# k and v held as two heads by 64 partitions instead of four heads by 32, in a two-stage attention followed by a token mixer

## The chip, the cores and the metric

The kernel runs on one core of a Trainium2 chip. The metric is the device time of the whole program in microseconds (us). Each kernel was run several times; a run is called fast here when it lies within 1.5% of the fastest run of the same kernel in the same call, and slow otherwise. The trace of the kernel before, from which its profile below is read, is of a run recorded as slow (165.15 us). Where ratios are quoted, they are the mean time of one kernel's fast runs over that of the other's fast runs of the same rounds, so they are not quite the ratio of the medians that stand beside them.

## The reference, cut to what matters

There are 8 batches, 8 heads, 576 positions and 64 channels per head, and 32 packed rows p per head.

```
p_packed = softmax(p k^T / 8) v          # 32 x 64 per head: "packed" rows
attn     = softmax(q p_packed^T / 8) p_packed   # 576 x 64 per head
x        = heads side by side            # 576 x 512 per batch
W_tok    = (x w_q)(x w_k)^T / 8          # 576 x 576
out      = relu(W_tok x) w_out           # float32
```

The change touches the first line only: the scores of the packed rows (p k^T) and the product of their softmax with v ("P times V").

## The kernel before

A batch goes through some twenty steps, and a fixed table decides the order in which the steps of neighbouring batches follow each other on every engine. k and v stand in SBUF with four heads on the 128 partitions: 32 partitions for each head, each with 18 consecutive rows, and the eight heads are two such groups G.

```python
NG, NP = 2, 4            # groups of heads, heads in a group
R, QP = 18, 32           # rows on a partition, partitions of a head
def rows(x, b):
    return x[b].rearrange("(G pos) (sh sl) d -> (pos sh) G sl d", G=NG, sl=R)

def sa(b, c):            # scores of the packed rows, one third c of the rows
    ...
    for r in range(NC3):
        for G in range(NG):
            for pos in range(NP):                        # one head at a time
                m = slice(pos * QP, (pos + 1) * QP)
                nc.tensor.matmul(ps[m, r, G], kT[:, r, G, m], pT[:, b, G * NP + pos],
                                 start=True, stop=True)
    ...                                                  # e1 = exp(scale * ps)

def pv(b, _):            # P times V, one row of each partition at a time
    ...
    for s in range(R):
        e1, r, par = st[b]["e1", s // KR], s % KR // 2, s % 2
        for G in range(NG):
            for pos in range(NP):
                m = slice(pos * QP, (pos + 1) * QP)
                nc.tensor.matmul(
                    ps[m, G, 0:Dh + 1], e1[m, r, G, par, :], v_sb[m, G, s, 0:Dh + 1],
                    start=s == 0 and G == 0, stop=s == R - 1, skip_group_check=True)
    ...
```

In a batch that is 72 matmuls for the scores (128 rows by 32 columns of weights, 64 moving columns) and 144 for P times V (32 by 32, 65 moving columns). Each has a weight load of its own. I call a load and its matmul a pair; the program has 2904.

The softmax here doesn't subtract the row's maximum and nothing guards it: scores larger than these inputs give would overflow.

## Time and profile before

| | before |
|---|---|
| median of 3 runs (lowest to highest) | 165.62 us (163.43 to 167.62) |
| span of the profiled run | 163.3 us |
| TensorE busy | 127.2 us (78%) |
| stops of the weight loads at multiples of 128 pairs | 10, together 25.5 us |
| matmul time spent at half clock | 20.5 us |

These lines of the page of the kernel before give the busy time of each engine, then rows of 40 equal slices of the span (4.1 us each; a digit is the busy share in tenths, and PEclk is the granted TensorE clock in tenths of full speed), then the DMA queue that moves instructions (packets, MB, share of 16 engines' time).

```profile
span 163.3 us, 6603 instructions
PE 127.2 (78%) x2904; PEld 87.3 (53%) x2904; DVE 81.6 (50%) x198; ACT 86.5 (53%) x176; POOL 67.4 (41%) x90
...
PE   6652895984979795999079992999929969999950
PEclk9997589699999999999759999699975999999997
DMA  5999999999249969987963989675960241274874
...
q8 instruction: 22, 0.36, 1.0%
```

TensorE is the busiest engine, but the row has holes at slices 19, 24 and 29 (counted from 0), and PEclk falls to 5 to 7 at or just after them. The chain of work that ended last, followed back through the span, as shares by engine and then by line:

```profile
## 4 chain that ended last, share of the span: by engine, by line
PE 70%; issue 14%; DMA 5%; DVE 4%; SPq 2%; ACT 1%; DVEq 0%; ACTq 0%
PE out_ps L430 20%; PE T_ps L221 10%; PE pv_ps L269 7%; PE e_ps L318 6%; DMA v_in<-in_v_dram 5%; PE warm_ps L205 4%; PE mix_ps L399 4%; PE e_ps L256 3%; PE aT_ps L339 3%; PE wk_ps L347 3%; PE wq_ps L358 2%; PE g_ps L371 2%; PE y_ps L380 2%; SPq L133 1%; DVE rs L326 1%
```

So 14% of the span is "issue": the engine waited for nothing that the profile shows. The timeline of the weight loads (PEld) around the largest hole, in columns start, length, engine, line, operation, tile, count and the idle time before it:

```profile
76.82 0.24 PEld L269 LDWEIGHTS <-e_2148 32*32 32x32 bf16 x19
77.10 0.10 PEld L430 LDWEIGHTS <-rest 128*128 128x128 bf16 x1
82.71 0.10 PEld L430 LDWEIGHTS <-rest 128*128 128x128 bf16 x1 [5.51 <-issue]
82.72 0.12 PEld L339 LDWEIGHTS <-a_2068 96*128 96x128 bf16 x1
```

The same stretch for the matmuls (PE):

```profile
75.61 0.78 PE L269 MATMUL pv_ps<-v_bf_83,e_2049 32*32 32x65 bf16 x48
76.20 0.57 PE L269 MATMUL pv_ps<-v_bf_83,e_2121 32*32 32x65 bf16 x48
76.59 0.59 PE L269 MATMUL pv_ps<-v_bf_83,e_2148 32*32 32x65 bf16 x48
77.10 0.39 PE L430 MATMUL out_ps<-wout_w,rest 128*128 128x512 bf16 x1
82.71 0.61 PE L430 MATMUL out_ps<-wout_w,rest 128*128 128x512 bf16 x1 [5.22 <-issue]
```

The engine stops between two matmuls of one output step: both weight loads read the tile rest, which was complete, and still the second comes 5.6 us after the first. Just before, 144 pairs of P times V had gone by in 1.4 us. Sorted by start, the weight loads make ten stops over 1 us that are no wait for data. They come after the pairs in this table (counted from 0), and all numbers differ by multiples of 128, to within two. Two more pauses of the loads, after pairs 113 and 354 (1.0 and 2.4 us), read "issue" in the rows of the loads too, but the rows of their matmuls name a cast of v on GpSimd and one of wqk on VectorE as what ended them: those are waits for data, and both rows have to be read.

| after pair | 223 | 478 | 606 | 862 | 990 | 1246 | 1629 | 2013 | 2397 | 2653 |
|---|---|---|---|---|---|---|---|---|---|---|
| stop, us | 3.28 | 1.14 | 2.55 | 1.41 | 1.32 | 1.99 | 5.61 | 3.14 | 3.37 | 1.69 |

Three stretches of 20 us: busy time of PE, PEld, DVE, ACT and POOL in this order (with the number of instructions), then the clock, the DMA share and GB/s.

```profile
60.00:80.00 20.00, 15.66 (x517) 11.48 (x513) 11.68 (x29) 11.15 (x24) 10.30 (x14) 0.99 0.94 217
80.00:100.00 20.00, 16.34 (x383) 12.05 (x384) 11.09 (x27) 11.48 (x25) 7.36 (x9) 0.84 0.78 192
100.00:120.00 20.00, 16.56 (x384) 12.29 (x384) 11.51 (x27) 11.05 (x23) 6.67 (x8) 0.91 0.81 190
```

### The profile page before, as it was taken

To read this page: it belongs to the slowest core of one execution; us is meant where nothing else is said; L and a number is where in the kernel's file an instruction comes from. 1 tells how busy PE (TensorE), PEld (TensorE's weight loads), DVE (VectorE), ACT (ScalarE), POOL (GpSimd) and SP (SyncE) were. 2 spreads that over 40 slices of the span, in tenths; PEclk is the share of its full clock that TensorE was granted. 3 is DMA by queue.
4 is the path that set the end of the run, shared out by engine and by line. 5 is a ranking of instruction groups with operands and counts; after the bars stand their busy time and mean duration, and the time that the engine had idled before them with its cause. 6 is when DMAs were issued, how large, how long until landed. Compare 5 with 4: busy or idle time off the path is not lost.

```text
span 163.3 us, 6603 instructions
## 1 busy us (share of the span) xinstructions
PE 127.2 (78%) x2904; PEld 87.3 (53%) x2904; DVE 81.6 (50%) x198; ACT 86.5 (53%) x176; POOL 67.4 (41%) x90
## 2 busy tenths in 40 slices
PE   6652895984979795999079992999929969999950
PEld 2332673463758564866058681866727548565410
DVE  5220366143858583785026872667604747761310
ACT  3133455512955691885036863578514755877740
POOL 7730559900592494089000890068004450540000
PEclk9997589699999999999759999699975999999997
DMA  5999999999249969987963989675960241274874
GB/s 146 338 382 247 403 370 322 322 248 214 46 116 287 187 151 176 208 285 191 227 135 96 311 199 206 144 276 134 145 197 5 51 111 43 68 201 120 227 212 139
DMA packets 16076, 32.20 MB, mean 197 GB/s; under 512 B 2736, under 2 KB 6064, under 8 KB 16048
## 3 DMA queue, kind: packets, MB, share of 16 engines
q1 hardware_dynamic: 11856, 23.99, 46.9%
q0 software_dynamic: 4192, 7.80, 27.7%
q8 instruction: 22, 0.36, 1.0%
q14 instruction: 6, 0.05, 0.1%
HBM read 30.15 MB, written 9.44 MB: 242 GB/s over the span
## 4 chain that ended last, share of the span: by engine, by line
PE 70%; issue 14%; DMA 5%; DVE 4%; SPq 2%; ACT 1%; DVEq 0%; ACTq 0%
PE out_ps L430 20%; PE T_ps L221 10%; PE pv_ps L269 7%; PE e_ps L318 6%; DMA v_in<-in_v_dram 5%; PE warm_ps L205 4%; PE mix_ps L399 4%; PE e_ps L256 3%; PE aT_ps L339 3%; PE wk_ps L347 3%; PE wq_ps L358 2%; PE g_ps L371 2%; PE y_ps L380 2%; SPq L133 1%; DVE rs L326 1%
## 5 line engine op out<-in xcount | busy, mean ns | idle before, releaser
L430 PE MATMUL out_ps<-wout_w,relu 128*128 128x512 bf16 x128 | 35.3, 392 | 0.0
L120 ACT ACTIVATE o_sb<-out_ps 128x512 f32<-128x512 f32 x28 | 16.7, 595 | 15.0 <-PE out_ps L430 13.3
L312 DVE COPY qT<-T_ps 128x768 bf16<-128x768 bf16 x24 | 13.3, 555 | 13.2 <-PE T_ps L221 13.1
L247 DVE COPY kT<-T_ps 128x768 bf16<-128x768 bf16 x24 | 13.0, 546 | 11.7 <-PE T_ps L221 11.1
L205 PE MATMUL warm_ps<-warm 128*128 128x512 bf16 x40 | 17.2, 464 | 1.2 <-DVE warm L185 1.2
L430 PEld LDWEIGHTS <-relu 128*128 128x128 bf16 x128 | 11.6, 103 | 7.9 <-issue 0.9
L318 PEld LDWEIGHTS <-qT 128*96 128x96 bf16 x192 | 13.3, 142 | 4.6 <-issue 3.5
L390 ACT ACTIVATE relu<-mix_ps 128x512 bf16<-128x512 f32 x24 | 13.6, 605 | 2.2 <-PE mix_ps L399 1.9
L341 DVE COPY aT<-aT_ps 128x384 bf16<-128x384 bf16 x24 | 8.5, 353 | 11.9 <-PE aT_ps L339 11.9
L120 ACT ACTIVATE wk<-wk_ps 96x128 bf16<-96x128 f32 x16 | 4.3, 271 | 15.0 <-PE wk_ps L347 14.9
L399 PE MATMUL mix_ps<-wqT,y 128*128 128x512 bf16 x32 | 10.9, 389 | 0.1
L273 DVE RECIPROCAL rec<-pv_ps 128x2 f32<-128x2 f32 x8 | 1.4, 171 | 18.5 <-PE pv_ps L269 18.5
L282 POOL TENSOR_TENSOR ppb<-pp,mask 128x256 bf16<-128x256 bf16 x16 | 10.5, 679 | 0.1
L221 PE MATMUL T_ps<-ident,q_bf 128*128 128x128 bf16 x108 | 10.0, 235 | 0.0
L318 PE MATMUL e_ps<-ppT_115,qT 128*96 128x64 bf16 x96 | 7.4, 226 | 3.2 <-issue 3.2
L221 PE MATMUL T_ps<-ident,k_bf 128*128 128x128 bf16 x108 | 9.4, 225 | 0.0
L347 PEld LDWEIGHTS <-aT 128*96 128x96 bf16 x96 | 7.8, 134 | 2.6 <-issue 0.4
L430 PE MATMUL out_ps<-wout_w,rest 128*128 128x512 bf16 x16 | 5.0, 394 | 5.2 <-issue 5.2
L118 DVE COPY o_sb<-out_ps 128x512 f32<-128x512 f32 x8 | 5.4, 671 | 7.1 <-PE out_ps L430 3.7
L221 PEld LDWEIGHTS <-k_bf 128*128 128x128 bf16 x108 | 7.3, 101 | 2.7 <-issue 0.8
L347 PE MATMUL wk_ps<-pqk,aT 128*96 128x64 bf16 x96 | 8.3, 214 | 0.1
L256 PE MATMUL e_ps<-pT,kT 128*32 128x64 bf16 x576 | 8.1, 199 | 0.3 <-DVE kT L247 0.3
(320 smaller groups left out, 287.6 us busy)
## 6 DMA issues: line engine op xcount, KB each, us to landing
v_in<-in_v_dram SPq DMA_DIRECT2D x7, 1152.0 KB, 8.4
out_dram<-o_sb SPq DMA_DIRECT2D x24, 192.0 KB, 2.6
k_bf<-in_k_dram POOLq DMA_DIRECT2D x6, 576.0 KB, 10.3
q_bf<-in_q_dram POOLq DMA_DIRECT2D x6, 576.0 KB, 8.2
out_dram<-o_sb SPq DMA_DIRECT2D x24, 128.0 KB, 2.5
out_dram<-o_sb SPq DMA_DIRECT2D x24, 64.0 KB, 2.2
k_in<-in_k_dram SPq DMA_DIRECT2D x3, 384.0 KB, 3.9
v_in<-in_v_dram SPq DMA_DIRECT2D x3, 384.0 KB, 7.7
```

What stands on the lines that cost most here:

```text
L120: nc.scalar.activation(o, i, COPY)
L205: nc.tensor.matmul(ps, warm[:, 0:P], warm, start=True, stop=True)
L221: nc.tensor.transpose(ps[:, r, G, :], xc[:, G, r].rearrange("a x d -> a (x d)"), ident)
L247: nc.vector.tensor_copy(kT, ps)
L256: nc.tensor.matmul(ps[m, r, G], kT[:, r, G, m], pT[:, b, G * NP + pos], start=True, stop=True)
L269: nc.tensor.matmul(ps[m, G, 0:Dh + 1], e1[m, r, G, par, :], v_sb[m, G, s, 0:Dh + 1], start=s == 0 and G == 0, stop=s == R - 1, skip_group_ ...
L312: nc.vector.tensor_copy(qT, ps.rearrange("a r G (pos s) -> a (G pos) r s", s=QP))
L318: nc.tensor.matmul(ps[:, :, h, :], qT[:, h].rearrange("a r s -> a (r s)"), st[b]["ppT"][:, h], start=True, stop=True)
L347: nc.tensor.matmul(ps[:, par, :], st[b]["aT"][:, G, c, par, :], st[b]["pqk"][:, G, Dl:], start=G == 0, stop=G == NG - 1)
L390: nc.scalar.activation(o, i, RELU)
L399: nc.tensor.matmul(ps, yT[:, j * P:(j + 1) * P], wqT[:, 0:SM], start=True, stop=True)
L430: nc.tensor.matmul(ps, lhsT, wout_w[:, j, :], start=j == 0, stop=j == NJ - 1)
```

## The change

The intent is half as many matmuls in both steps. k and v are held as two heads by 64 partitions with nine rows each, in four groups of heads. A P-times-V matmul then contracts 64 rows instead of 32, and a score matmul makes 64 output partitions instead of 32; as before, it takes two rows of a partition at a time. q keeps its layout. The first loads of k and v come by head group (four pieces) instead of by thirds of the rows, and the first q in one piece.

```diff
+    RK, KP, KG = 9, 64, 4
+    NF = KG * RK // NC3
+    NT = NF // 2
...
-    def rows(x, b):
-        return x[b].rearrange("(G pos) (sh sl) d -> (pos sh) G sl d", G=NG, sl=R)
+    shape = {"q": [P, NG, R, Dh], "k": [P, KG, RK, Dh], "v": [P, KG, RK, Dh]}
+    def rows(name, b):
+        return src[name][b].rearrange("(G pos) (sh sl) d -> (pos sh) G sl d",
+                                      G=shape[name][1], sl=shape[name][2])
...
     def sa(b, c):
-        for r in range(NC3):
-            for G in range(NG):
-                for pos in range(NP):
-                    m = slice(pos * QP, (pos + 1) * QP)
-                    nc.tensor.matmul(ps[m, r, G], kT[:, r, G, m], pT[:, b, G * NP + pos],
-                                     start=True, stop=True)
+        for t in range(NT):
+            for pos in range(2):
+                m = slice(pos * KP, (pos + 1) * KP)
+                h0, h1 = (2 * ((c * NF + 2 * t + x) // RK) + pos for x in range(2))
+                nc.tensor.matmul(ps[m, t], kT[:, t, m],
+                                 heads[:, 2 * h0:2 * h1 + 2:2 * (h1 - h0) + 1],
+                                 start=True, stop=True)
...
     def pv(b, _):
-        for s in range(R):
-            e1, r, par = st[b]["e1", s // KR], s % KR // 2, s % 2
-            for G in range(NG):
+        for g in range(NG):
+            for s in range(RK):
                 for pos in range(NP):
-                    m = slice(pos * QP, (pos + 1) * QP)
+                    h = NP * g + pos
+                    m = slice(h % 2 * KP, (h % 2 + 1) * KP)
+                    f = h // 2 * RK + s
                     nc.tensor.matmul(
-                        ps[m, G, 0:Dh + 1], e1[m, r, G, par, :], v_sb[m, G, s, 0:Dh + 1],
-                        start=s == 0 and G == 0, stop=s == R - 1, skip_group_check=True)
+                        ps[pos * L:(pos + 1) * L, g, 0:Dh + 1],
+                        st[b]["e1", f // NF][m, f % NF // 2, f % 2, :], v_sb[m, f, 0:Dh + 1],
+                        start=s == 0 and g == 0, stop=s == RK - 1, skip_group_check=True)
```

The pairs fall from 2904 to 2040.

More of the change, by code (lines that the diff above doesn't have):

```diff
@@ L54 @@
     R, QP = 18, 32
+    RK, KP, KG = 9, 64, 4
     NC3 = 3
+    NF = KG * RK // NC3
+    NT = NF // 2
     CH = S // (2 * NC3)
-    KR = R // NC3
+    QR = R // NC3
     VW = Dh + 2
@@ L120, in copy, with load, load_cast @@
             nc.scalar.activation(o, i, COPY)
-    def rows(x, b):
-        return x[b].rearrange("(G pos) (sh sl) d -> (pos sh) G sl d", G=NG, sl=R)
+    shape = {"q": [P, NG, R, Dh], "k": [P, KG, RK, Dh], "v": [P, KG, RK, Dh]}
+    src = {"q": q, "k": k, "v": v}
     x_in = {}
-    def load(x, name, b, pieces=1):
-        x_in[name, b] = t = two.tile([P, NG, R, Dh], fp32, tag=name + "_in", name=name + "_in")
-        n = R // pieces
-        for c in range(pieces):
-            nc.sync.dma_start(t[:, :, c * n:(c + 1) * n], rows(x, b)[:, :, c * n:(c + 1) * n])
-    def load_cast(x, name, b):
-        x_in[name, b] = t = three.tile([P, NG, R, Dh], bf16, tag=name + "_bf", name=name + "_bf")
-        nc.gpsimd.dma_start(t, rows(x, b))
+    def rows(name, b):
+        return src[name][b].rearrange("(G pos) (sh sl) d -> (pos sh) G sl d",
+                                      G=shape[name][1], sl=shape[name][2])
+    def load(name, b, pieces=None):
+        x_in[name, b] = t = two.tile(shape[name], fp32, tag=name + "_in", name=name + "_in")
+        for o in pieces or [slice(None)]:
+            nc.sync.dma_start(t[o], rows(name, b)[o])
+    def load_cast(name, b):
+        x_in[name, b] = t = three.tile(shape[name], bf16, tag=name + "_bf", name=name + "_bf")
+        nc.gpsimd.dma_start(t, rows(name, b))
     def cast(act, o, i):
@@ L144, in cast @@
             nc.gpsimd.tensor_copy(o, i)
-    NF, NV = 2, 3
-    v_bufs = [const.tile([P, NG, R, VW], bf16, name=f"v_bf{i}") for i in range(NV)]
+    NL, NV = 2, 3
+    v_bufs = [const.tile([P, KG * RK, VW], bf16, name=f"v_bf{i}") for i in range(NV)]
     p_first = const.tile([P, 4, Dh], fp32)
@@ L157 @@
     nc.sync.dma_start(p_first, p_v[:, 0])
-    for x, name in ((k, "k"), (v, "v"), (q, "q")):
-        load(x, name, 0, NC3)
+    by_head = [(slice(None), G) for G in range(KG)]
+    load("k", 0, by_head)
+    load("v", 0, by_head)
+    load("q", 0)
     for i, w in enumerate((moe_w_q, moe_w_k)):
@@ L162 @@
                           w.rearrange("(h d) c -> d h c", d=Dh))
-    for x, name in ((k, "k"), (v, "v"), (q, "q")):
-        load(x, name, 1)
+    for name in "kvq":
+        load(name, 1)
     pT = const.tile([P, B, H, 2, L], bf16)
@@ L188, in constants @@
         for t in v_bufs:
-            nc.vector.memset(t[:, :, :, Dh:], 1.0)
+            nc.vector.memset(t[:, :, Dh:], 1.0)
         for t in ppT_bufs:
@@ L214, with transposes, flat @@
     rests = {}
-    def transposes(xc):
-        ps = psum(tp_pool, [P, NC3, NG, P], bf16, "T_ps")
-        for r in range(NC3):
-            for G in range(NG):
-                nc.tensor.transpose(ps[:, r, G, :],
-                                    xc[:, G, r].rearrange("a x d -> a (x d)"), ident)
-        return ps
+    def transposes(blocks):
+        ps = psum(tp_pool, [P, NT, P], bf16, "T_ps")
+        for t, block in enumerate(blocks):
+            nc.tensor.transpose(ps[:, t, :], block, ident)
+        return ps
+    def flat(x, c):
+        return x.rearrange("a G s d -> a (G s) d")[:, c * NF:(c + 1) * NF]
     def vc(b, c):
-        sl = slice(c * KR, (c + 1) * KR)
-        cast(act_vc[c], v_bufs[b % NV][:, :, sl, 0:Dh], x_in["v", b][:, :, sl])
+        cast(act_vc[c], v_bufs[b % NV][:, c * NF:(c + 1) * NF, 0:Dh], flat(x_in["v", b], c))
     def kc(b, c):
-        if b < NF:
-            st[b]["k", c] = t = three.tile([P, NG, NC3, 2, Dh], bf16, tag="k_c", name="k_c")
-            cast(act_kc[c], t.rearrange("a G r x d -> a G (r x d)"),
-                 x_in["k", b][:, :, c * KR:(c + 1) * KR].rearrange("a G s d -> a G (s d)"))
+        if b < NL:
+            st[b]["k", c] = t = three.tile([P, NF, Dh], bf16, tag="k_c", name="k_c")
+            cast(act_kc[c], t, flat(x_in["k", b], c))
     def qc(b, c):
-        if b < NF:
+        if b < NL:
             st[b]["q", c] = t = three.tile([P, NG, NC3, 2, Dh], bf16, tag="q_c", name="q_c")
@@ L243, in kt @@
     def kt(b, c):
-        ps = transposes(st[b]["k", c] if b < NF else
-                        x_in["k", b].rearrange("a G (c r x) d -> a c G r x d", c=NC3, x=2)[:, c])
-        st[b]["kT", c] = kT = four.tile([P, NC3, NG, P], bf16, tag="kT", name="kT")
+        xk = st[b]["k", c] if b < NL else flat(x_in["k", b], c)
+        ps = transposes([xk[:, 2 * t:2 * t + 2].rearrange("a x d -> a (x d)")
+                         for t in range(NT)])
+        st[b]["kT", c] = kT = four.tile([P, NT, P], bf16, tag="kT", name="kT")
         nc.vector.tensor_copy(kT, ps)
@@ L250, in sa @@
         kT = st[b]["kT", c]
-        ps = psum(sc_pool, [P, NC3, NG, 2, L], fp32, "e1_ps")
-        for r in range(NC3):
-            for G in range(NG):
-                for pos in range(NP):
-                    m = slice(pos * QP, (pos + 1) * QP)
-                    nc.tensor.matmul(ps[m, r, G], kT[:, r, G, m], pT[:, b, G * NP + pos],
-                                     start=True, stop=True)
-        st[b]["e1", c] = e1 = six.tile([P, NC3, NG, 2, L], bf16, tag="e1", name="e1")
+        heads = pT[:, b].rearrange("a h x l -> a (h x) l")
+        ps = psum(sc_pool, [P, NT, 2, L], fp32, "e1_ps")
+        for t in range(NT):
[5 more added lines that the diff above has]
+                                 start=True, stop=True)
+        st[b]["e1", c] = e1 = six.tile([P, NT, 2, L], bf16, tag="e1", name="e1")
         nc.scalar.activation(e1, ps, EXP, scale=scale)
@@ L263, in pv @@
         ps = psum(w_pool, [P, NG, VW], fp32, "pv_ps")
-        for s in range(R):
-            e1, r, par = st[b]["e1", s // KR], s % KR // 2, s % 2
-            for G in range(NG):
+        for g in range(NG):
+            for s in range(RK):
                 for pos in range(NP):
-                    m = slice(pos * QP, (pos + 1) * QP)
+                    h = NP * g + pos
+                    m = slice(h % 2 * KP, (h % 2 + 1) * KP)
+                    f = h // 2 * RK + s
                     nc.tensor.matmul(
-                        ps[m, G, 0:Dh + 1], e1[m, r, G, par, :], v_sb[m, G, s, 0:Dh + 1],
-                        start=s == 0 and G == 0, stop=s == R - 1, skip_group_check=True)
+                        ps[pos * L:(pos + 1) * L, g, 0:Dh + 1],
+                        st[b]["e1", f // NF][m, f % NF // 2, f % 2, :], v_sb[m, f, 0:Dh + 1],
+                        start=s == 0 and g == 0, stop=s == RK - 1, skip_group_check=True)
         rec = two.tile([P, NG, 1], fp32, tag="rec", name="rec")
@@ L308, in qt @@
     def qt(b, c):
-        ps = transposes(st[b]["q", c] if b < NF else
-                        x_in["q", b].rearrange("a G (r c x) d -> a c G r x d", c=NC3, x=2)[:, c])
+        xq = (st[b]["q", c] if b < NL else
+              x_in["q", b].rearrange("a G (r c x) d -> a c G r x d", c=NC3, x=2)[:, c])
+        ps = transposes([xq[:, G, r].rearrange("a x d -> a (x d)")
+                         for r in range(NC3) for G in range(NG)])
         st[b]["qT", c] = qT = four.tile([P, H, NC3, QP], bf16, tag="qT", name="qT")
-        nc.vector.tensor_copy(qT, ps.rearrange("a r G (pos s) -> a (G pos) r s", s=QP))
+        nc.vector.tensor_copy(qT, ps.rearrange("a (r G) (pos s) -> a (G pos) r s", G=NG, s=QP))
     def sc(b, c):
@@ L410, in store @@
     def store(b, t0, o):
-        o_v = out[b].rearrange("(n m) d -> m n d", m=KR)
+        o_v = out[b].rearrange("(n m) d -> m n d", m=QR)
         t, end = t0, t0 + o.shape[0]
@@ L446, in lk @@
     def lk(b, _):
-        if b == NF:
+        if b == NL:
             nc.gpsimd.dma_start(p_nat[:, 1:], p_v[:, 1:])
-        if b >= NF:
-            load_cast(k, "k", b)
+        if b >= NL:
+            load_cast("k", b)
     def lv(b, _):
-        if b >= NF:
-            load(v, "v", b)
+        if b >= NL:
+            load("v", b)
     def lq(b, _):
-        if b >= NF:
-            load_cast(q, "q", b)
-        if b == NF:
+        if b >= NL:
+            load_cast("q", b)
+        if b == NL:
             nc.gpsimd.dma_start(wout_w, moe_w_out.rearrange("(j r) c -> r j c", r=P))
```

## The prediction

> **What bounds the kernel now.** TensorE. The page shows it 78% busy in a span of 163.3 us; the chain that ended last is 70% TensorE work plus 14% "issue", time in which it waited for nothing the profile names. VectorE, ScalarE and GpSimd are at 50, 53 and 41%. The DMA engines are full only for the first 37 us.
>
> I read the "issue" share as instruction fetch. In the list of weight-load starts there are ten stops of 1.1 to 5.6 us, 25.5 us together, and every one lies a multiple of 128 load-matmul pairs after the first (pair 223, 478, 606, 862, 990, 1246, 1629, 2013, 2397, 2653). The instruction queue moved 22 packets of 16 KB. [...] Most stops end 2.3 to 2.5 us after a fetch begins, and a fetch often begins 1.1 us after a block is entered: a block used up in under 3.5 to 5 us stops the engine. P times V (144 pairs in 1.2 us) and the packed scores (72 pairs) do that nearly every batch. Longer stops are followed by stretches at half clock, 3.4 to 6.8 us each.
>
> **What the change removes.** 288 of 576 score pairs and 576 of 1152 P-times-V pairs: 2904 to 2040 pairs, 30%.
> - P times V: the starts come in fours every 29 ns, four 32-row tiles at once [...]. After: 64 rows by 32 columns, still four column groups, half as many fours. I expect 29 ns per four again: 1.15 to 0.6 us per batch, 4.5 us in all.
> - Scores: four 32-column tiles take 29 ns per transposed block. Two 64-column tiles should take 29 to 31 ns per block (two 64-column loads hide under 55 ns in the transposes of p). No gain in array time, only in instructions.
> - Fetch: replaying the weight-load times with the pairs removed and 3.5 to 5 us per block, stops fall from 9 to 23 us (same model, before) to 0 to 3 us. I expect 2 to 7 us to remain, and fewer half-clock stretches, worth 2 us.
>
> **What it adds.** k and v rows in DRAM become 2304 bytes instead of 4608: twice the packets. In the trace, 4608 bytes took 181 ns and 2048 bytes 86 ns, so v costs no more; the cast loads of k go from 192 ns for 2304 written bytes to perhaps 2 x 108 ns, some 2.5 us of DMA time in all. The first scores wait for half of k(0) instead of a third, about 0.5 us.
>
> **Sum.** -4.5 (P times V) -20 (stops) -2 (clock) +1; some 5 us comes back as waits for loads and for VectorE and ScalarE, whose work is unchanged: 165.6 - 20.6 = 145 us. Range 137 to 154. Faster 0.95, same 0.04, slower 0.01.
>
> **What would show it.** P-times-V bursts of 72 pairs in 0.6 us; score bursts of unchanged length; "issue" in the chain from 14% to under 6%; 15 or 16 fetch packets; kT, exp and cast groups unchanged.
>
> **What would make it wrong.** Two row groups keep weight loads from overlapping (P times V still 1.1 us); the stops persist because fetches start late for another reason; loads become the limit and take the gain back.

Its sum is -4.5 - 20 - 2 + 1 + 5 = -20.5 us, which gives 145 us. A block there is 128 pairs, as the stops are spaced in the trace; 2904 pairs and 22 packets of 16 KB make 132 pairs to a packet. The 3.5 to 5 us that a block has to last are the author's estimate from the figures just before it: 1.1 us until a fetch begins and 2.3 to 2.5 us from there to the end of the stop make about 3.5 us; for the 5 us it gives no figures. The trace bears it out in part. Of the 20 blocks between the first stop and pair 2780, counted without the stops, six of the seven that lasted under 3.5 us ended in a stop of over 1 us, two of the four between 3.5 and 5 us, and one of the nine longer ones. A fetch began 1.1 us into three of these blocks; for the others it began between 0.8 us before and 5.9 us after the block was entered.

## The result, and the profile after

The changed kernel took 133.35 us (median of 4 runs, 132.47 to 136.27) beside 165.25 us for the kernel before (4 runs, 163.43 to 167.62). The ratio of the fast runs is 0.8082, with a 95% interval of 0.7963 to 0.8201. The time lies 3.65 us under the lower end of the predicted range. The page of the changed kernel (a slice is now 3.3 us):

```profile
span 130.9 us, 4877 instructions
PE 116.0 (89%) x2040; PEld 78.6 (60%) x2040; DVE 80.8 (62%) x198; ACT 86.1 (66%) x176; POOL 67.8 (52%) x90
...
PE   5796299499996999999999999999999999999920
PEclk9999859959999999999999999999999999999995
DMA  4999999999999999799999999999953431765784
...
q8 instruction: 16, 0.26, 0.8%
```

The holes are gone from slice 13 on, the clock stays at full speed from slice 9 to the last one, and 16 instruction packets were fetched instead of 22. The DMA row is now full from slice 1 to slice 28 but for one, yet from 40 us on TensorE waits for no load. The chain below has 7% of waiting for the first q, at the start. The chain that ended last:

```profile
## 4 chain that ended last, share of the span: by engine, by line
PE 77%; DMA 7%; ACT 3%; SPq 3%; DVE 2%; issue 2%; POOL 1%; ACTq 0%
PE out_ps L444 24%; PE T_ps L228 12%; DMA q_in<-in_q_dram 7%; PE e_ps L332 7%; PE warm_ps L213 5%; PE mix_ps L413 5%; PE e_ps L265 4%; PE aT_ps L353 4%; PE wk_ps L361 3%; PE pv_ps L280 3%; PE wq_ps L372 3%; SPq L139 3%; PE g_ps L385 2%; PE y_ps L394 1%; PE pqk_ps L315 1%
```

"Issue" fell from 14% to 2%. The three stretches of 20 us from 60 to 120 us:

```profile
60.00:80.00 20.00, 20.00 (x434) 14.32 (x431) 15.61 (x39) 16.09 (x35) 13.88 (x18) 1.00 1.09 311
80.00:100.00 20.00, 20.00 (x354) 14.41 (x350) 16.02 (x37) 16.05 (x34) 10.08 (x12) 1.00 0.91 232
100.00:120.00 20.00, 19.76 (x300) 12.51 (x299) 12.68 (x32) 15.69 (x35) 6.79 (x9) 1.00 0.46 123
```

TensorE is busy without a gap for 40 us and nearly so for another 20. In the kernel before it was busy for 15.7 to 16.6 of each 20 us, part of it at a lower clock.

From the records of both traces the change of the span can be split into four parts. The stops at multiples of 128 pairs sum to 25.5 us before and 1.3 us after (one stop, after pair 606). TensorE's busy time fell by 11.2 us (127.2 to 116.0). Of that, P times V is 4.5 us: the distances from start to start inside its bursts sum to 9.42 us before and 4.90 us after. The other 6.7 us fit the clock: 20.5 us of matmul time lay in half-clock stretches before and 6.8 us after, and half of the difference is 6.9 us. (In those stretches a 128-column transpose of q or k mostly starts 106 to 108 ns after the one before it, outside them 55 to 57 ns, so about half of that time is the lower clock.) The idle time of TensorE outside the stops rose by 3.0 us (10.6 to 13.6), if the stops are measured as above, from one start of a weight load to the next. In sum, -24.2 - 4.5 - 6.7 + 3.0 = -32.4 us, which is the change of the span (163.3 to 130.9 us).

The score bursts did not become shorter: their start-to-start distances sum to 4.31 us before and 4.52 us after. The group of score matmuls shows half as many instructions for the same busy time. Before:

```profile
L247 DVE COPY kT<-T_ps 128x768 bf16<-128x768 bf16 x24 | 13.0, 546 | 11.7 <-PE T_ps L221 11.1
L256 PE MATMUL e_ps<-pT,kT 128*32 128x64 bf16 x576 | 8.1, 199 | 0.3 <-DVE kT L247 0.3
```

After:

```profile
L255 DVE COPY kT<-T_ps 128x768 bf16<-128x768 bf16 x24 | 13.0, 546 | 6.7 <-PE T_ps L228 5.7
L265 PE MATMUL e_ps<-pT,kT 128*64 128x64 bf16 x288 | 8.3, 201 | 0.2 <-DVE kT L255 0.2
```

The copy of kT beside it is unchanged, as the same data passes.

### The profile page after: what moved, and what is told of

It reads as the page before. It is cut to its first block, busy times and chain, and to the rows that moved or that the text cites. A ratio compares the mean times of both kernels' runs of the same rounds, so it can differ in the third digit from the quotient of the medians.

```text
span 130.9 us, 4877 instructions
## 1 busy us (share of the span) xinstructions
PE 116.0 (89%) x2040; PEld 78.6 (60%) x2040; DVE 80.8 (62%) x198; ACT 86.1 (66%) x176; POOL 67.8 (52%) x90
## 4 chain that ended last, share of the span: by engine, by line
PE 77%; DMA 7%; ACT 3%; SPq 3%; DVE 2%; issue 2%; POOL 1%; ACTq 0%
PE out_ps L444 24%; PE T_ps L228 12%; DMA q_in<-in_q_dram 7%; PE e_ps L332 7%; PE warm_ps L213 5%; PE mix_ps L413 5%; PE e_ps L265 4%; PE aT_ps L353 4%; PE wk_ps L361 3%; PE pv_ps L280 3%; PE wq_ps L372 3%; SPq L139 3%; PE g_ps L385 2%; PE y_ps L394 1%; PE pqk_ps L315 1%
## 5 line engine op out<-in xcount | busy, mean ns | idle before, releaser
L444 PE MATMUL out_ps<-wout_w,relu 128*128 128x512 bf16 x128 | 33.9, 379 | 0.0
L326 DVE COPY qT<-T_ps 128x768 bf16<-128x768 bf16 x24 | 13.3, 555 | 9.7 <-PE T_ps L228 9.3
L444 PEld LDWEIGHTS <-relu 128*128 128x128 bf16 x128 | 11.2, 99 | 7.4 <-issue 0.4
L332 PEld LDWEIGHTS <-qT 128*96 128x96 bf16 x192 | 11.6, 128 | 1.3 <-issue 0.2
L413 PE MATMUL mix_ps<-wqT,y 128*128 128x512 bf16 x32 | 10.6, 381 | 0.1
L228 PE MATMUL T_ps<-ident,q_bf 128*128 128x128 bf16 x108 | 9.1, 219 | 1.1 <-issue 1.1
L265 PE MATMUL e_ps<-pT,kT 128*64 128x64 bf16 x288 | 8.3, 201 | 0.2 <-DVE kT L255 0.2
L361 PEld LDWEIGHTS <-aT 128*96 128x96 bf16 x96 | 7.0, 124 | 2.2 <-DVE aT L355 0.2
L228 PEld LDWEIGHTS <-q_bf 128*128 128x128 bf16 x108 | 7.0, 100 | 2.0 <-issue 1.5
L265 PEld LDWEIGHTS <-kT 128*64 128x64 bf16 x288 | 6.2, 113 | 3.3 <-DVE kT L255 1.1
L361 PE MATMUL wk_ps<-pqk,aT 128*96 128x64 bf16 x96 | 7.7, 207 | 0.0
L342 DVE RECIPROCAL rr<-rs 96x16 f32<-96x16 f32 x24 | 6.0, 249 | 1.8
```

Of the source, the lines that this page charges most:

```text
L228: nc.tensor.transpose(ps[:, t, :], block, ident)
L265: nc.tensor.matmul(ps[m, t], kT[:, t, m], heads[:, 2 * h0:2 * h1 + 2:2 * (h1 - h0) + 1], start=True, stop=True)
L326: nc.vector.tensor_copy(qT, ps.rearrange("a (r G) (pos s) -> a (G pos) r s", G=NG, s=QP))
L332: nc.tensor.matmul(ps[:, :, h, :], qT[:, h].rearrange("a r s -> a (r s)"), st[b]["ppT"][:, h], start=True, stop=True)
L361: nc.tensor.matmul(ps[:, par, :], st[b]["aT"][:, G, c, par, :], st[b]["pqk"][:, G, Dl:], start=G == 0, stop=G == NG - 1)
L413: nc.tensor.matmul(ps, yT[:, j * P:(j + 1) * P], wqT[:, 0:SM], start=True, stop=True)
```

## The experiments

The theory, read from the stops and the instruction packets of the first trace, is that most of the gain comes from feeding TensorE fewer instructions: it stops when it uses up a block of 128 pairs faster than the next one is fetched. The first rival is that the array time in P times V is most of it. The second is that the new layout of k and v (larger first pieces, casts over contiguous rows, other packets) earns it. The third, among those who accept the fetch, is that only the number of pairs counts, not how densely they come.

All variants below are built on the changed kernel except where said. Each call ran its kernels and the kernel before on one chip. "Stops" are gaps of over 0.8 us between weight loads at a multiple of 128 pairs, from the profiled run; gaps at such a place that are a wait for data are left out. The traced runs of a2, a3 and a4 are slow (a4: 163.16 us, beside 157.87 us for its fast run), those of a6, a7 and b1 fast. "Half clock" is the time at half clock up to the last weight load.

| kernel | pairs | stops | half clock, us | median, us | fast runs, mean |
|---|---|---|---|---|---|
| before (first trace) | 2904 | 10, 25.5 us | 27.3 | 165.25 | 164.6 |
| changed (first trace) | 2040 | 1, 1.3 us | 6.8 | 133.35 | 133.1 |
| a2: scores in 32 columns | 2328 | 3, 5.7 us | 10.2 | 137.64 | 137.1 |
| a4: P times V in half columns | 2616 | 8, 20.4 us | 34.1 | 160.98 | 157.9 (one run) |
| a3: both | 2904 | 10, 27.4 us | 23.9 | 165.37 | 160.9 (one run) |
| a6: P times V with twice the columns | 2040 | 2, 2.1 us | 3.4 | 135.91 | 135.5 |
| a7: other matmuls in quarters | 2568 | 4, 5.9 us | 10.2 | 141.61 | 141.8 |
| b1: before, half of P times V left out | 2328 | 4, 5.4 us | 6.8 | 138.81 | 138.5 |

In the call of a2, a4, a3 and a6 the kernel before had a median of 163.71 us (7 runs, 160.68 to 167.61; one counts as fast, 160.68). In the call of a7 and b1 it had 165.41 us (fast runs 161.36 and 163.54), and the changed kernel was run again as a control:

> The changed kernel unaltered, as a control on the chip of this call: 132 to 136 us, at most two stops at multiples of 128 pairs.

It took 135.21 us (133.08 to 137.33; fast runs 134.94 and 133.08). The ratio of fast runs was 0.8249 (0.7906 to 0.8592). Its trace shows no stop at a multiple of 128 pairs. Its start was slower than that of the first trace: the chain has 14% of waiting for the first k. A difference of 2 us between calls is therefore nothing to explain. The call of a2, a4, a3 and a6 had no control of its own.

### a2: the scores back in 32-column pieces

```diff
-            for pos in range(2):
-                m = slice(pos * KP, (pos + 1) * KP)
+            for i in range(4):
+                pos = i // 2
+                m = slice(i * QP, (i + 1) * QP)
```

> The changed kernel with its score matmuls cut back to four 32-column tiles per transposed block: 288 more pairs (2328), same array time. Fetch theory (the gain is mostly fewer TensorE instructions): some stops at multiples of 128 pairs come back, 3 to 10 us of them, 136 to 145 us. Rival, the gain is array time in P times V and the new row layout in DRAM: no change, 133 to 135 us.

It took 137.64 us, with three stops of 5.7 us together. The score bursts took no longer than in the changed kernel (4.21 us in sum, against 4.52). So the score half of the change earns its few us (2.4 to 4.1 between fast runs, depending on the call of the changed kernel that it is set beside) through the instructions alone, as expected.

### a4 and a6: the same work cut into more pairs, and more work in the same pairs

a4 cuts each P-times-V matmul into 33 and 32 moving columns. The result is the same.

```diff
-                for pos in range(NP):
+                for i in range(2 * NP):
+                    a, pos = i // NP, i % NP
+                    n0, n1 = [0, 32, 65][a:a + 2]
...
-                        ps[pos * L:(pos + 1) * L, g, 0:Dh + 1],
-                        st[b]["e1", f // NF][m, f % NF // 2, f % 2, :], v_sb[m, f, 0:Dh + 1],
-                        start=s == 0 and g == 0, stop=s == RK - 1, skip_group_check=True)
+                        ps[pos * L:(pos + 1) * L, g, n0:n1],
+                        st[b]["e1", f // NF][m, f % NF // 2, f % 2, :], v_sb[m, f, n0:n1],
+                        start=s == 0 and g == 0 and a == 0, stop=s == RK - 1, skip_group_check=True)
```

> The changed kernel with each P-times-V matmul cut into 33 and 32 moving columns: 576 more pairs (2616), the same columns through the array, the same result. Fetch theory: bursts of 144 pairs again, stops of 10 to 20 us in all, 143 to 158 us. Rival (array time and layout): at most 134 to 137 us.

a6 keeps the pairs and repeats the 65 moving columns, into a part of PSUM that nothing reads.

```diff
-        ps = psum(w_pool, [P, NG, VW], fp32, "pv_ps")
+        wide = psum(w_pool, [P, NG, 2, VW], fp32, "pv_ps")
+        ps = wide[:, :, 0, :]
...
-                        ps[pos * L:(pos + 1) * L, g, 0:Dh + 1],
+                        wide[pos * L:(pos + 1) * L, g, :, 0:Dh + 1],
...
-                        v_sb[m, f, 0:Dh + 1],
+                        v_sb[m, f:f + 1, 0:Dh + 1].to_broadcast((KP, 2, Dh + 1)),
```

> The changed kernel with 130 moving columns in each P-times-V matmul (the second 65 a repeat that goes to unused PSUM): pairs unchanged at 2040, array time of P times V as before the change, about 56 ns per four instead of 29. Fetch theory: bursts of 72 pairs last 1.05 us instead of 0.57, no stops, +4 us, 136 to 139 us. Rival, that P times V array time was the larger part: +10 us or more.

The two make a better pair than I had planned, because the half-width matmuls of a4 turned out no faster than whole ones. The bursts of P times V sum to 9.15 us in a4 and 8.25 us in a6 (4.90 in the changed kernel). So both spend nearly the same array time on it and give the same result; what differs is 2616 pairs against 2040. The times are 160.98 and 135.91 us. The page and the chain of a4 (some matmul records are missing from its trace and from that of a6, which is why PE counts fewer than PEld):

```profile
span 161.4 us, 6006 instructions
PE 126.2 (78%) x2593; PEld 89.0 (55%) x2616; DVE 81.4 (50%) x198; ACT 86.6 (54%) x176; POOL 67.6 (42%) x90
...
PE   6664299648989299869995897999939969999950
PEclk9998559955899857999999699999996999999995
```

```profile
## 4 chain that ended last, share of the span: by engine, by line
PE 69%; issue 14%; DMA 6%; ACT 4%; SPq 2%; DVE 1%; ACTq 0%
```

The same of a6:

```profile
span 134.0 us, 4854 instructions
PE 117.2 (87%) x2017; PEld 81.7 (61%) x2040; DVE 83.7 (62%) x198; ACT 86.5 (65%) x176; POOL 67.7 (51%) x90
...
PE   5299958698987999999999999999999999999920
PEclk9999999779999999999999999999999999999995
```

```profile
## 4 chain that ended last, share of the span: by engine, by line
PE 71%; DMA 13%; ACT 5%; SPq 3%; issue 3%; DVE 0%; ACTq 0%
```

a4 has the holes, the low clocks and the 14% of "issue" of the kernel before; a6 has almost none. A doubled array time in P times V costs about 1 to 3 us (135.91 against 133.35 to 135.21 us in the other calls); the pairs cost some 25 us (medians; 22 us between the fast runs, of which a4 has one). That falsifies the first rival. For a6 I had expected 136 to 139 us and no stop; it took a little less and had two stops. The median of a4 lies 3 us over the 143 to 158 us that I expected; its one fast run, 157.87 us, lies within. That the halved matmuls of a4 save no time is read from the traces alone: about 8 ns from start to start on average, for 32 and 33 columns in a4 and for 65 in the changed kernel.

A more literal undo of P times V, with 32-row weights in the new layout, was not run: two matmuls of different row tiles would then add into the same PSUM partitions, and no run here shows what that gives. In the kernel before and in the changed one each of these output quarters belongs to one row tile.

### a3: as many pairs as before, in the new layout

The edits of a2 and a4 together.

> Both of the above: 2904 pairs as in the kernel before, with the new row layout, loads and casts. Fetch theory: stops of 20 to 27 us and half-clock stretches after them, 158 to 168 us, within a few us of the kernel before. If the DRAM layout or the order of the first loads earned something, it stays clearly under that, at 140 to 155 us.

It took 165.37 us beside 163.71 us for the kernel before (one fast run each, 160.9 and 160.68). The ten stops stand after the same pair numbers as in the kernel before (223, 478, 606, 862, 990, 1246, 1629, 2013, 2397, 2653) and sum to 27.4 us. So the new layout, the other first loads and the other casts together earn nothing that can be seen. This falsifies the second rival.

### b1: fewer pairs in the old layout

The kernel before, with every second step of P times V left out. Its output is wrong, which doesn't matter for the time.

```diff
-        for s in range(R):
+        for s in range(0, R, 2):
...
-                        start=s == 0 and G == 0, stop=s == R - 1, skip_group_check=True)
+                        start=s == 0 and G == 0, stop=s == R - 2, skip_group_check=True)
```

> The kernel before the change with every second P-times-V step left out (a wrong result on purpose): 2328 pairs, old layout in DRAM. Fetch theory: stops fall to 3 to 8 us, 134 to 141 us, like the changed kernel with 32-column scores (2328 pairs, 137.6 us). If the new layout is needed for the gain: 145 us or more.

It took 138.81 us (ratio of fast runs 0.8525, 0.8345 to 0.8705), close to a2, which has the same 2328 pairs in the new layout (137.64 us). Two thirds of the removed pairs thus give most of the gain without any change of layout. This run also drops array time, so alone it would not tell the fetch from the array; a6 does that.

### a7: more pairs, spread

Every 512-column matmul of the output projection and of the mixing step is cut into four of 128 columns.

```diff
-            nc.tensor.matmul(ps, lhsT, wout_w[:, j, :], start=j == 0, stop=j == NJ - 1)
+            for n in range(4):
+                w = slice(n * P, (n + 1) * P)
+                nc.tensor.matmul(ps[:, w], lhsT, wout_w[:, j, w], start=j == 0 and n == 0,
+                                 stop=j == NJ - 1, skip_group_check=True)
... (the mixing matmul likewise)
```

> The changed kernel with every 512-column matmul (output projection, mixing) cut into four of 128 columns: 528 more pairs (2568, nearly the 2616 of the kernel with halved P-times-V columns), but at 56 ns a pair, outside the dense bursts. If it is the rate at which pairs are used up that stops the engine: hardly a stop, +1 to +4 us for the extra loads, 134 to 138 us. If the number of pairs or of fetched blocks alone decides: 155 to 162 us as with the halved columns.

It took 141.61 us, beside 135.21 us for the changed kernel and 160.98 us for a4, which has about as many pairs. Its four stops sum to 5.9 us. So density does matter: nearly the same number of pairs costs 5.9 us in stops when it is spread and 20.4 us when it comes in bursts. But "hardly a stop" was wrong, and 141.6 us lies over the 134 to 138 expected: the number of pairs matters too. Both fit the reading that a block has to last long enough, which no run here tests by itself. In the changed kernel P times V comes round every 12.5 us with 255 pairs, so a block lasts 6.3 us on average; in a7, at that pace, it would last 5.0 us, and in a4 4.9 us. The averages of a7 and a4 are alike, so what tells them apart is that in a4 144 of the pairs go by in 1.1 to 1.2 us.

### Two faster versions

v1 leaves out the warm-up matmul that follows each early step (31 of 40), and v2 only the six of batch 1.

```diff
 v1
             steps[name](b, c)
-            if (b, name) in early:
-                warm_up(1)
 v2
-    early |= {(1, "kt"), (1, "sa")}
```

> The changed kernel without the warm-up matmul after each early step of batches 0 and 1 (31 of the 40 warm-up matmuls, 5% of the chain): an attempt at a faster version. Without them the chain is shorter by up to 4 us, but the clock may stay at half through the first 30 us: 129 to 135 us.

v1 took 132.23 us (fast runs 132.38 on average, against 134.01 for the control of that call). The two were then repeated with five rounds, with v2 and a control.

> The changed kernel unaltered again, five rounds, to compare the two versions below with on the same chip: 132 to 136 us.

> No warm-up matmuls after the early steps, again: 131.5 to 133 us, 1 to 2% under the changed kernel of the same call, if the difference of the last call (134.0 and 132.4 us in fast runs) was real; equal within 0.5% if it was chance.

> The changed kernel with the warm-ups of batch 0 kept and the six of batch 1 left out (they stand on the chain between 26 and 29 us): 1 to 2 us under the changed kernel, and not behind the version without any, since the clock of the first 25 us stays up: 131 to 133 us.

The control took 134.85 us, v1 131.94 us and v2 132.67 us (medians of 6 runs; means of the fast runs 134.75, 131.94 and 132.61). v1 is 2.1% under the changed kernel (131.94 / 134.75 = 0.979) and has the lowest time of all; v2 is not better, against my expectation. That expectation took the clock of the first 25 us to stay up; in the first trace of the changed kernel, with all warm-ups, it is at half from 15.6 to 19.0 us and from 25.8 to 29.3 us, 6.8 us in all. In the profiled run of v1 in the earlier call the clock was at half for 17.1 us, from 14.5 to 31.5 us, and the kernel was still faster: there, keeping the clock up costs more than it brings.

## Why the prediction was wrong

What held:
- **The bound and its cause.** TensorE set the time (78% busy before, 89% after), and its "issue" share fits instruction fetch: the instruction queue moved 22 packets of 16 KB for 2904 pairs and 16 for 2040, 132 and 128 pairs to a packet, and each of the ten stops of the kernel before ended 2.3 to 3.1 us after such a packet began. Every stop of TensorE over 0.8 us that the rows of the matmuls put down to nothing else, in every variant, lies at a multiple of 128 pairs to within two, though the code at these places differs.
- **P times V.** Predicted -4.5 us, measured -4.5 us. Four matmuls of 64 by 32 overlap as four of 32 by 32 did: 7.8 to 7.9 ns a matmul in the steady bursts of the changed kernel (mostly 29 to 33 ns from four to four), 7.8 to 8.1 ns before, in all bursts but the first (distances over 200 ns left out).
- **Scores.** No gain in array time: 4.31 and 4.52 us.
- **DMA packets.** The cast loads of k went to 107 ns for 1152 bytes (108 predicted); loads in 2304-byte packets take 93 ns, in line with 181 ns for 4608.
- **The signs to look for.** "Issue" under 6% (it is 2%) and 16 packets of instructions (15 or 16 predicted).

What failed is the sum "-4.5 -20 -2 +1 and some 5 us comes back", in three terms. Two are sizes of effects that were foreseen; the third, that loads and the other engines would take time back, did not happen.
- **The clock, -2 us predicted, about -6.7 measured.** I had counted the stretches of half clock and not the matmul time inside them: 20.5 us, which costs about half of that (106 to 108 ns from transpose to transpose there, 55 to 57 ns elsewhere). In the kernel before, the stop from 77.1 to 82.7 us passes into half clock from 79.5 to 86.3 us, and that from 118.3 to 121.7 us into half clock from 120.5 to 127.3 us. Up to the last weight load the stretches last 6.8 us three times and 3.4 us twice in the kernel before, and 3.4 us twice in the changed one. TensorE was not idle all through the time before them: in the 3.4 us before the half clock of 79.5, 103.4 and 120.5 us it was busy for 41 to 43%. That the stops bring the low clock is read from the order in time, over all traces. After the first 40 us, each of the ten stops of 2.3 us or more was followed by half clock within 4.6 us of its start, only one of the 29 shorter ones was (1.97 us, in a7), and until the last weight load half clock began nowhere else. In the first 32 us it also follows waits for data, in the changed kernel too (the loads wait from 12.6 to 15.5 us for a cast of q, and half clock begins at 15.6 us). What the clock was worth, apart from the stops, no run measures: 6.7 us is what is left of the busy time.
- **The stops, -20 predicted, -24.2 measured**, from start to start as predicted. The replay with the pairs removed had said 0 to 3 us would remain, and 1.3 us did. I put 2 to 7 us there, out of caution.
- **What comes back, +6 us predicted (1 + 5), +3.0 measured.** I expected loads and the other engines to become the limit. TensorE is busy for 20.00, 20.00 and 19.76 of 20 us from 60 to 120 us, so nothing was given back there. Even the 3.0 us are mostly in the way a stop is measured: from start to start it takes in the tail of the last matmul. Counted as idle time of TensorE, the stops fell by 21.7 us (22.8 to 1.1) and the idle time outside them rose by 0.5 us only (13.3 to 13.8; in the first 40 us 6.7 to 7.7).

The three misses add up to 4.7 + 4.2 + 3.0 = 11.9 us, the difference between the predicted and the measured change of the span (-20.5 and -32.4 us). Counted as idle time they are 4.7 + 1.7 + 5.5, and what did not come back is the largest. In short, the stops were worth more than their own length, and no other engine and no load took the time back, although the DMA engines were about full (share 1.09 and 0.91 from 60 to 100 us). The prediction calls them full only for the first 37 us of the kernel before; its DMA row shows 9 in many later slices as well.

What stays open is why a fetch begins when it does. In the ten stops of the kernel before, the engine went on 2.3 to 3.1 us after the fetch began. But in the changed kernel a fetch began between 0.6 and 4.0 us after a block was entered (once the first loads were over; in the last three blocks, by the same count, at that moment or up to 1.8 us before it), and in the largest stop of the kernel before it began 3.2 us into the stop, in the first one 0.2 us. No run here shows what sets this delay.

## What to carry to other kernels

When the chain shows "issue" on TensorE, sort the weight loads by start and look at the pair numbers at which they stop. Here these differed by multiples of 128 pairs (ten stops, 25.5 of 163.3 us), which I read as an engine short of instructions, and the count of small matmuls was a cost of its own, beside their time in the array: a4 against a6 puts 22 to 25 us on 576 pairs at nearly the same array time (9.15 and 8.25 us). In such a case try fewer and larger matmuls even where the array time stays the same, first where small ones come in bursts (20.4 us of stops in a4, 5.9 us in a7 with nearly as many pairs, spread). Count also the work done at half clock after such stops, which here was worth about 6.7 us, more than the removed array time (4.5 us).
